# Windowed attention and two gated products on one core: scores three units ahead, weight conversions placed behind later landings, last output tile in two halves

## The chip, the cores and the metric

One core of a Trainium2 chip. The metric is the time of one execution on the device in microseconds, lower is better; three runs of the kernel before took 643.66 to 646.2 us, median 645.15.

## What is computed

```python
def reference(q, k, v, n_global, n_local, moe_w_a, moe_w_b, moe_w_out, moe2_w1, moe2_w2, moe2_w3, moe2_w_out):
    # q, k, v: (2, 8, 768, 64); n_global 8, n_local 96
    scores = q @ k.T / sqrt(64) - slope[h] * dist      # kept where global or in the last 96 keys
    a = softmax(where(keep, scores, -1e9))
    x = rows of (a @ v)                                # (1536, 512)
    x = (x @ w_a) * (x @ w_b) @ w_out                  # d_ff 1536
    return ((x @ w1) * (x @ w2) @ w3) @ w_out2         # d_ff 1024, out (1536, 512) float32
```

Only 104 earlier keys and the 128 of a query tile's own block can count, so a tile's scores are 232 wide, or 128 for the first tile of a batch.

## The kernel before

Weights reach the core as 64-bit floats and are turned into pairs of tiles, a high and a low part in TensorE's own 32-bit format; each product is three matmuls (high by high, high by low, low by high; lines 192 to 194).

**Attention** runs in 24 units (NU), a unit being four heads of one query tile of 128 rows. A unit passes scores (S, line 622 on PE), bias and row maximum (line 554 on VectorE), exponential with row sum (558, ScalarE), reciprocal (580, 581, VectorE), scaling (563, POOL), transposes (T, line 630 on PE), their copy out of PSUM, half by ScalarE (597) and half by VectorE (599), values (V, 641 on PE), and the split of the result into x high and x low (608 on ScalarE, 609 on VectorE). Twelve e tiles, two qk tiles, two vv tiles and one set of score banks serve all units. The first four units are 128 wide, the others 232. In step i of the generator `attention` (line 687) PE gets V of unit i-1, T of unit i and S of unit i+2; up to step 8 each for itself, after that the three in one block.

**Products.** x is cut into three chunks of 512 rows, eight units each. The first stage has six groups of 256 hidden columns, the second four. For a group and a chunk, `gate` makes 48 matmuls (two halves, weights A and B), `gated` forms the product on ScalarE and VectorE (721 to 729), and `down` makes 24 matmuls, whose results VectorE adds up (765). The order is chunk by chunk for groups 0 and 1, then group by group. The first product needs units 0 to 7 and weight A of group 0. In the second stage w3 and the last weight are multiplied first (`fold`, 24 matmuls, line 815), as they become ready.

**Weights.** `prep` (446) takes a raw buffer (three while attention lasts, two after it), loads 1 MB through SP's queue (455) and converts it: shift on VectorE (463), clamp on POOL (464), scale on ScalarE (465), two merges on VectorE (466, 468), high part on ScalarE (472), low part on VectorE (473), after which the buffer is free. Group 0 loads at once; group 1 when more than GP = 8 units have had their scores; later groups when attention has ended and their slot comes free.

**The order of work** is made beforehand by `Plan`, a list scheduler: every step is a strand that yields an engine, a planned duration and a time from which it is ready, and the planner always places the step that can start first, the lower rank first among equals (attention 8, a unit's softmax from 10 up, products 20, weights from 30 up). All instructions are then issued in order of their planned start, and each engine runs its own in that order. A load is planned at 3.1 us on the DMA engine plus 2.2 us; eight transposes at 0.1 + 0.87 x 2 = 1.84 us.

The last tile of each output is added up on VectorE and sent by SP's queue (777).

Of the kernel before, what the change touches and what calls it, by code (L numbers as in the profile page):

```python
# [10 lines left out]
I32 = mybir.dt.int32  # L11
AF = mybir.ActivationFunctionType
ALU = mybir.AluOpType
PSUM = bass.MemoryType.PSUM

P = 128
# [87 lines left out]
def op(eng, dur, ready, fn):  # L104
    return ((eng, dur),), ready, fn
# [3 lines left out]
def attention_moe_moe_kernel(  # L109
# [14 lines left out]
    nc = tc.nc  # L124
# [3 lines left out]
    B, NQ, _, NP, _ = qk.shape  # L128
    D = P // 2
    H = 2 * NP  # L130
    S = NQ * P
# [7 lines left out]
    CH = 512  # L139
    NC = NT // CH  # L140
# [242 lines left out]
    D_DVE = lambda n: 0.16 + 0.00104 * n  # L383
    D_MM = lambda n: 0.227 * n / 512
    LAT = 0.1
    PELAT = 0.25
    GP = 8
    with ExitStack() as fast:
        fast.enter_context(tc.manual_schedule())
        pl = Plan()  # L390
# [52 lines left out]
            return op("DMA", 3.1 * mb, 0.0, fn)  # L443


        def prep(src, shape, dst, key, gate=lambda: 0.0):

            yield gate
            i, t = yield from raw.get()
            buf = raw.tiles[i]  # L450
            if src.dtype == F32:
                w = buf.rearrange("p f w -> p (f w)")[:, 0:1024].bitcast(F32)
                t = (yield op("DMA", 1.6, t, lambda: nc.sync.dma_start(w.rearrange("p (a f) -> p a f", a=shape[0]), src))) + 2.2
            else:
                t = (yield op("DMA", 3.1, t, lambda: nc.sync.dma_start(
                    buf.rearrange("p f w -> p (f w)"), src.bitcast(I32).rearrange("p a f -> p (a f)")))) + 2.2
                low, top = buf[:, :, 0], buf[:, :, 1]
                tf = top.bitcast(F32)
                w = low.bitcast(F32)

                c = yield op("DVE", 0.75, t, lambda: nc.vector.tensor_scalar(low, low, 29, None, ALU.logical_shift_right))  # L463
                a = yield op("POOL", 1.2, t, lambda: nc.gpsimd.tensor_scalar(tf, tf, F64_MAX, -F64_MAX, ALU.min, ALU.max))  # L464
                a = yield op("ACT", D_ACT(1024), a + LAT, lambda: nc.scalar.activation(tf, tf, AF.Copy, scale=2.0 ** -112))  # L465
                c = yield op("DVE", 1.25, max(a, c) + LAT, lambda: nc.vector.scalar_tensor_tensor(  # L466
                    low, top, 3, low, ALU.logical_shift_left, ALU.bitwise_or))
                t = yield op("DVE", 1.25, c + LAT, lambda: nc.vector.scalar_tensor_tensor(  # L468
                    low, top, -0x80000000, low, ALU.bitwise_and, ALU.bitwise_or))
            w2 = w.rearrange("p (a f) -> p a f", a=shape[0])  # L470
            free = yield (lambda: slot_of(key))
            t = yield op("ACT", D_ACT(1024), max(t, free) + LAT, lambda: nc.scalar.activation(dst()[0], w2, AF.Copy))  # L472
            t = yield op("DVE", 1.25, t + LAT, lambda: nc.vector.tensor_tensor(  # L473
                dst()[1], w2, dst()[0].bitcast(F32), ALU.subtract))
            raw.free[i] = t + LAT
            ready[key] = t + LAT
# [26 lines left out]
            n0 = 2 if tag == "O" else KD  # L503
            return [s[:, 2 * k + z, :].rearrange("p (a f) -> p a f", a=n0) for z in range(2)]

        def prep_group(st, g, rank, gate=lambda: 0.0):
            for k, tag in enumerate("ABO" if st == 1 else "AB"):
                src = ((w_a, w_b, w_o) if st == 1 else (w_1, w_2))[k][g]
                pl.spawn(prep(src, (2, DM) if tag == "O" else (KD, 256), lambda tag=tag: slot(st, g, tag),
                              (tag, st, g), gate), rank)  # L510

        order = [(b, t) for t in range(NQ) for b in range(B)]
        NU = 2 * len(order)
        xr = {}
        att = {"began": 0, "done": 0, "end": 0.0}
        sS = [[bk[:, 0:2 * KW].rearrange("p (u k) -> p u k", u=2) for bk in bank[0:2]]][0]
        pts = bank[2:4]
        po = bank[4][:, 0:2 * P].rearrange("p (u k) -> p u k", u=2)  # L520
# [123 lines left out]
        def attention():  # L644

            def part(what, num):

                w, blocks = width(num)
                nb = len(blocks)
                if what == "S":  # L650
                    def r():
                        if ("q", num) not in ev or (num and ("ttr", num - 1) not in ev):
                            return None
                        return max(ev["q", num][1], ev.get(("ttr", num - 1), 0.0))

                    def then(t):
                        att["began"] += 1
                        if num % 2:
                            qkb.free[ev["q", num][0]] = t + LAT
                        pl.spawn(softmax(num, [t - 0.24 * nb + PELAT, t + PELAT]), 8)  # L660
                    return r, 0.3 + 0.34 * nb, lambda: scores(num), then
                if what == "T":
                    def r():
                        if ("e", num) not in ev or (num and ("pT", num - 1) not in ev):
                            return None
                        return max(ev["e", num][0], ev.get(("pT", num - 1), 0.0))

                    def then(t):
                        _, es, k = ev["e", num]
                        for ei in es:  # L670
                            eb.free[ei] = t + LAT
                        stb.free[k] = t
                        pl.spawn(evicted(num, [t - 0.44 * nb, t]), 9)
                    return r, 0.1 + 0.87 * nb, lambda: transposes(num), then

                def r():
                    if ("pT", num) not in ev or ("v", num) not in ev or (num and ("x", num - 1) not in ev):
                        return None
                    return max(ev["pT", num], ev["v", num][1], ev.get(("x", num - 1), 0.0))

                def then(t):
                    if num % 2:
                        vvb.free[ev["v", num][0]] = t + LAT
                    pl.spawn(rows(num, t), 9)
                return r, 0.2 + 0.54 * nb, lambda: values(num), then

            for i in range(-2, NU + 1):
                ps = [part(w, n) for w, n in (("V", i - 1), ("T", i), ("S", i + 2)) if 0 <= n < NU]
                whole = i > 8
                for k in range(1 if whole else len(ps)):  # L690
                    now = ps if whole else ps[k:k + 1]
                    t = 0.0
                    for x in now:
                        t = max(t, (yield x[0]))

                    def fn(now=now):
                        for x in now:
                            x[2]()

                    t = yield op("PE", sum(x[1] for x in now), t, fn)  # L700
                    for x in reversed(now):
                        x[3](t)
                        t -= x[1]
# [4 lines left out]
        accr = {}  # L708
# [46 lines left out]
        def added(st, g, c, m, k, t):  # L755

            last = g == (G1 if st == 1 else G2) - 1
            po = ybank.tiles[k]
            a = lambda: (accs[c] if c < 2 else late["acc"])[:, m, :]
            if g == 0:  # L760
                r = (yield lambda: late.get("t")) if c == 2 else 0.0
                r = max(r, accr.get((c, m), 0.0))
                u = yield op("ACT", D_ACT(CH), max(t + PELAT, r), lambda: nc.scalar.activation(a(), po, AF.Copy))
            else:
                u = yield op("DVE", D_DVE(CH), max(t + PELAT, accr[c, m]), lambda: nc.vector.tensor_tensor(a(), a(), po, ALU.add))  # L765
            ybank.free[k] = u + LAT
            accr[c, m] = u + LAT
            if last and st == 1:
                tok = slice(c * CH, (c + 1) * CH)
                u = yield op("ACT", D_ACT(CH), u + LAT, lambda: nc.scalar.activation(xh[:, m, tok], a(), AF.Copy))  # L770
                u = yield op("DVE", D_DVE(CH), u + LAT, lambda: nc.vector.tensor_tensor(
                    xl[:, m, tok], a(), xh[:, m, tok].bitcast(F32), ALU.subtract))
                xr[2, c, m] = accr[c, m] = u + LAT
            if last and st == 2:
                b, t = order[4 * c + m]
                row = (b * NQ + t) * P
                yield op("DMA", 0.8, u + LAT, lambda: nc.sync.dma_start(out[row:row + P, :], a()))
# [96 lines left out]
        pl.spawn(attention(), 8)  # L874
        pl.spawn(switch(), 0)
        prep_group(1, 0, 30)
        prep_group(1, 1, 31, lambda: 0.0 if att["began"] > GP else None)
        for g in range(2, G1):
            prep_group(1, g, 30 + g, lambda g=g: late.get("t") if ("A", 1, g - 2) in users else None)
            if g < 6:  # L880
# [17 lines left out]
    with tc.If(fv > 0):  # L898
        with ExitStack() as pg:
# [9 lines left out]
            for b in range(B):  # L909
                for p in range(NP):  # L910
# [9 lines left out]
                    for t in range(NQ):  # L920
# [12 lines left out]
                        po = gT.tile([P, P], F32, tag="O", name=f"o{nm}_{t}", bufs=1)  # L933
                        for j in range(2):
# [13 lines left out]
                            st = gs.tile([P, 4], F32, tag="st", name=f"st{nm}_{t}{j}")  # L948
# [14 lines left out]
        with ExitStack() as pg:  # L963
# [3 lines left out]
            f = ffn("g")  # L967
# [72 lines left out]
```

## Time and profile before

| | us |
|---|---|
| median of three runs | 645.15 |
| the profiled execution | 646.13 |
| its span in the trace | 644.2 |
| PE busy | 617.1 |
| DVE busy | 396.0 |
| ACT busy | 249.9 |
| POOL busy | 105.0 |

The span runs from the first to the last instruction; the 1.9 us to the execution's time lie around it. PE is TensorE, DVE VectorE, ACT ScalarE, SP the engine whose queue issues the loads. Lines (L622) are those of the kernel. A wait is put down to what came last before the waiting instruction. A busy row of several matmuls counts from the start of the first to the modelled end of the last, which overlaps the next by a little.

### The profile page before, as it was taken

What the parts mean: (1) busy time and instruction counts of PE and PEld (TensorE: products, weight loads), DVE (VectorE), ACT (ScalarE), POOL (GpSimd) and SP (SyncE); (2) the same over time, 40 slices, a digit from 0 to 9 for tenths busy, and PEclk for the clock granted to TensorE, in tenths of its full rate; (3) what the DMA queues carried; (4) which work ended last, traced back from release to release, by engine and by line L of the source; (5) the groups of instructions that cost most, each with busy time, mean ns of one, the idle gap of its engine ahead of it and who ended that gap; (6) DMA issues with size and microseconds to landing.
All of it is one profiled execution on the core that took longest, in us unless ns stands there. A gap on an engine that the chain in (4) does not pass through costs nothing.

```text
span 644.2 us, 8087 instructions
## 1 busy us (share of the span) xinstructions
PE 617.1 (96%) x3072; PEld 499.5 (78%) x3072; DVE 396.0 (61%) x693; ACT 249.9 (39%) x486; POOL 105.0 (16%) x149
## 2 busy tenths in 40 slices
PE   2788999999999999999999999999999999999996
PEld 1456777778888888888888888888888888888884
DVE  5979856555377997758788544981375276323333
ACT  4765766652244434413434223542452133111110
POOL 4645333330012121101111000110011010000000
PEclk9987999999999999999999999999999999999998
DMA  8454332320033433303333000420340030000012
GB/s 329 143 210 176 119 112 83 132 108 2 0 131 131 136 125 132 131 0 131 130 132 131 1 0 23 160 79 1 93 169 0 1 131 2 1 0 1 33 66 102
DMA packets 11647, 57.79 MB, mean 90 GB/s; under 512 B 1360, under 2 KB 2384, under 8 KB 6736
## 3 DMA queue, kind: packets, MB, share of 16 engines
q1 hardware_dynamic: 11456, 57.19, 25.4%
q8 instruction: 26, 0.43, 0.3%
q14 instruction: 21, 0.17, 0.1%
q10 hardware_dynamic: 144, 0.00, 0.0%
HBM read 54.04 MB, written 3.15 MB: 89 GB/s over the span
## 4 chain that ended last, share of the span: by engine, by line
PE 92%; DVE 3%; DMA 2%; POOL 1%; issue 1%; SPq 0%; ACT 0%; ACTq 0%
PE bank L192 28%; PE bank L194 28%; PE bank L193 28%; PE bank L630 3%; PE bank L641 3%; PE bank L622 2%; DMA raw<-in_moe_w_a_dram 2%; POOL e L563 1%; DVE e L554 1%; DVE st L580 1%; DVE raw L463 0%; SPq L529 0%; DVE slot L473 0%; DVE pT L599 0%; DVE acc L765 0%
## 5 line engine op out<-in xcount | busy, mean ns | idle before, releaser
L192 PE MATMUL bank<-xh,slot 128*128 128x512 f32 x480 | 188.3, 392 | 0.0
L193 PE MATMUL bank<-xl,slot 128*128 128x512 f32 x480 | 186.9, 389 | 0.0
L194 PE MATMUL bank<-xh,slot 128*128 128x512 f32 x480 | 186.8, 389 | 0.0
L464 POOL TENSOR_SCALAR raw<-raw 128x1024 f32<-128x1024 f32 x38 | 52.5, 1381 | 355.6 <-DMA raw<-in_moe_w_dram 157.4
L765 DVE TENSOR_TENSOR acc<-acc,bank 128x512 f32<-128x512 f32 x96 | 65.7, 684 | 70.0 <-PE bank L194 69.8
L192 PEld LDWEIGHTS bank<-xh,slot 128*128 128x128 f32 x480 | 90.2, 188 | 21.6 <-issue 3.2
L194 PEld LDWEIGHTS bank<-xh,slot 128*128 128x128 f32 x480 | 90.1, 188 | 19.0
L193 PEld LDWEIGHTS bank<-xl,slot 128*128 128x128 f32 x480 | 90.3, 188 | 18.3
L724 DVE TENSOR_TENSOR gt<-gt,bank 128x512 f32<-128x512 f32 x60 | 41.1, 684 | 68.5 <-PE bank L194 68.5
L728 ACT ACTIVATE gh<-gt 128x512 fp32r<-128x512 f32 x60 | 37.8, 630 | 115.1 <-DVE gt L724 115.1
L721 ACT ACTIVATE gt<-bank 128x512 f32<-128x512 f32 x60 | 35.8, 596 | 89.3 <-PE bank L194 89.1
L563 POOL TENSOR_SCALAR e<-e,st 128x232 f32<-128x232 f32 (+1 forms) x96 | 49.2, 531 | 65.3 <-DVE st L581 28.1
L465 ACT ACTIVATE raw<-raw 128x1024 f32<-128x1024 f32 x38 | 43.6, 1151 | 35.7 <-POOL raw L464 35.5
L192 PE MATMUL bank<-gh,slot 128*128 128x512 f32 x144 | 56.7, 394 | 0.0
L193 PE MATMUL bank<-gl,slot 128*128 128x512 f32 x144 | 56.2, 390 | 0.0
L194 PE MATMUL bank<-gh,slot 128*128 128x512 f32 x144 | 56.0, 389 | 0.0
L466 DVE SCALAR_TENSOR_TENSOR raw<-raw 128x1024 int32<-128x1024 int32 x38 | 47.8, 1259 | 9.2 <-ACT raw L465 8.8
L558 ACT ACTIVATE e<-e,st 128x232 f32<-128x232 f32 (+1 forms) x96 | 44.4, 464 | 21.3 <-DVE st L554 21.3
L729 DVE TENSOR_TENSOR gl<-gt,gh 128x512 fp32r<-128x512 f32 x60 | 44.9, 749 | 6.9 <-ACT gh L728 6.8
L468 DVE SCALAR_TENSOR_TENSOR raw<-raw 128x1024 int32<-128x1024 int32 x38 | 48.5, 1275 | 0.4
L472 ACT ACTIVATE slot<-raw 128x1024 fp32r<-128x1024 f32 x26 | 29.5, 1134 | 33.6 <-PE bank L193 23.8
L473 DVE TENSOR_TENSOR slot<-raw,slot 128x1024 fp32r<-128x1024 f32 x26 | 32.7, 1257 | 14.4 <-ACT slot L472 14.2
(67 smaller groups left out, 733.8 us busy)
## 6 DMA issues: line engine op xcount, KB each, us to landing
raw<-in_moe_w_dram SPq DMA_DIRECT2D x16, 1024.0 KB, 4.8
raw<-in_moe_w_out_dram SPq DMA_DIRECT2D x10, 1024.0 KB, 4.9
qk<-in_qk_dram SPq DMA_DIRECT2D x10, 720.0 KB, 4.2
raw<-in_moe_w_a_dram SPq DMA_DIRECT2D x6, 1024.0 KB, 5.6
raw<-in_moe_w_b_dram SPq DMA_DIRECT2D x6, 1024.0 KB, 6.5
vv<-in_vv_dram SPq DMA_DIRECT2D x10, 512.0 KB, 3.8
out_dram<-acc SPq DMA_DIRECT2D x12, 256.0 KB, 2.0
qk<-in_qk_dram SPq DMA_DIRECT2D x4, 256.0 KB, 4.1
```

The costliest lines, as they stand in the source:

```text
L192: nc.tensor.matmul(po, sh, mh, start=first, stop=False)
L193: nc.tensor.matmul(po, sh, ml, start=False, stop=False)
L194: nc.tensor.matmul(po, sl, mh, start=False, stop=last)
L464: a = yield op("POOL", 1.2, t, lambda: nc.gpsimd.tensor_scalar(tf, tf, F64_MAX, -F64_MAX, ALU.min, ALU.max))
L465: a = yield op("ACT", D_ACT(1024), a + LAT, lambda: nc.scalar.activation(tf, tf, AF.Copy, scale=2.0 ** -112))
L466: c = yield op("DVE", 1.25, max(a, c) + LAT, lambda: nc.vector.scalar_tensor_tensor(low, top, 3, low, ALU.logical_shift_left, ALU.bitwise_or))
L468: t = yield op("DVE", 1.25, c + LAT, lambda: nc.vector.scalar_tensor_tensor(low, top, -0x80000000, low, ALU.bitwise_and, ALU.bitwise_or))
L558: a = yield op("ACT", D_ACT(w) + 0.28, a + LAT, lambda: nc.scalar.activation(e, e, AF.Exp, bias=nmx, scale=-1.0, accum_out=sm))
L563: res["e"].append((yield op("POOL", 0.3 + 0.0011 * e.shape[1], r, lambda: nc.gpsimd.tensor_scalar(e, e, rs, 1.0, ALU.mult, ALU.mult))) + LAT)
L724: a = yield op("DVE", D_DVE(CH), max(a + LAT, pb), lambda: nc.vector.tensor_tensor(gt, gt, res["pB"], ALU.mult))
L729: a = yield op("DVE", D_DVE(CH), a + LAT, lambda: nc.vector.tensor_tensor(gl, gt, gh.bitcast(F32), ALU.subtract))
L765: u = yield op("DVE", D_DVE(CH), max(t + PELAT, accr[c, m]), lambda: nc.vector.tensor_tensor(a(), a(), po, ALU.add))
```

## The change

In `attention` PE gets S of unit i+3 in step i, and starts three units ahead. In `prep` a load of 64-bit weights is reckoned to land 5.5 us after its planned transfer instead of 2.2, and a new gate, `hold`, can keep the conversion back after the load. Group 1 uses it: its loads are no longer held, its conversions wait until GP = 7 units are through, and their rank is 12 instead of 31. In `added` the last output tile is added up and sent in two halves of 256 columns, the first by ScalarE's queue and the second by SP's.

```diff
--- before.py
+++ after.py
@@ -384,7 +384,7 @@
     D_MM = lambda n: 0.227 * n / 512
     LAT = 0.1
     PELAT = 0.25
-    GP = 8
+    GP = 7
     with ExitStack() as fast:
         fast.enter_context(tc.manual_schedule())
         pl = Plan()
@@ -443,7 +443,7 @@
             return op("DMA", 3.1 * mb, 0.0, fn)
 
 
-        def prep(src, shape, dst, key, gate=lambda: 0.0):
+        def prep(src, shape, dst, key, gate=lambda: 0.0, hold=lambda: 0.0):
 
             yield gate
             i, t = yield from raw.get()
@@ -453,7 +453,8 @@
                 t = (yield op("DMA", 1.6, t, lambda: nc.sync.dma_start(w.rearrange("p (a f) -> p a f", a=shape[0]), src))) + 2.2
             else:
                 t = (yield op("DMA", 3.1, t, lambda: nc.sync.dma_start(
-                    buf.rearrange("p f w -> p (f w)"), src.bitcast(I32).rearrange("p a f -> p (a f)")))) + 2.2
+                    buf.rearrange("p f w -> p (f w)"), src.bitcast(I32).rearrange("p a f -> p (a f)")))) + 5.5
+                yield hold
                 low, top = buf[:, :, 0], buf[:, :, 1]
                 tf = top.bitcast(F32)
                 w = low.bitcast(F32)
@@ -503,11 +504,11 @@
             n0 = 2 if tag == "O" else KD
             return [s[:, 2 * k + z, :].rearrange("p (a f) -> p a f", a=n0) for z in range(2)]
 
-        def prep_group(st, g, rank, gate=lambda: 0.0):
+        def prep_group(st, g, rank, gate=lambda: 0.0, hold=lambda: 0.0):
             for k, tag in enumerate("ABO" if st == 1 else "AB"):
                 src = ((w_a, w_b, w_o) if st == 1 else (w_1, w_2))[k][g]
                 pl.spawn(prep(src, (2, DM) if tag == "O" else (KD, 256), lambda tag=tag: slot(st, g, tag),
-                              (tag, st, g), gate), rank)
+                              (tag, st, g), gate, hold), rank)
 
 
 
@@ -684,8 +685,8 @@
                     pl.spawn(rows(num, t), 9)
                 return r, 0.2 + 0.54 * nb, lambda: values(num), then
 
-            for i in range(-2, NU + 1):
-                ps = [part(w, n) for w, n in (("V", i - 1), ("T", i), ("S", i + 2)) if 0 <= n < NU]
+            for i in range(-3, NU + 1):
+                ps = [part(w, n) for w, n in (("V", i - 1), ("T", i), ("S", i + 3)) if 0 <= n < NU]
                 whole = i > 8
                 for k in range(1 if whole else len(ps)):
                     now = ps if whole else ps[k:k + 1]
@@ -761,6 +762,17 @@
                 r = (yield lambda: late.get("t")) if c == 2 else 0.0
                 r = max(r, accr.get((c, m), 0.0))
                 u = yield op("ACT", D_ACT(CH), max(t + PELAT, r), lambda: nc.scalar.activation(a(), po, AF.Copy))
+            elif last and (st, c, m) == (2, NC - 1, 3):
+
+                b, n = order[4 * c + m]
+                row = (b * NQ + n) * P
+                for i in range(2):
+                    h = slice(i * (CH // 2), (i + 1) * (CH // 2))
+                    q = (nc.scalar, nc.sync)[i]
+                    u = yield op("DVE", D_DVE(CH // 2), max(t + PELAT, accr[c, m]), lambda h=h: nc.vector.tensor_tensor(
+                        a()[:, h], a()[:, h], po[:, h], ALU.add))
+                    yield op(("ACT", "DMA")[i], 0.3, u + LAT, lambda h=h, q=q: q.dma_start(out[row:row + P, h], a()[:, h]))
+                return
             else:
                 u = yield op("DVE", D_DVE(CH), max(t + PELAT, accr[c, m]), lambda: nc.vector.tensor_tensor(a(), a(), po, ALU.add))
             ybank.free[k] = u + LAT
@@ -874,7 +886,7 @@
         pl.spawn(attention(), 8)
         pl.spawn(switch(), 0)
         prep_group(1, 0, 30)
-        prep_group(1, 1, 31, lambda: 0.0 if att["began"] > GP else None)
+        prep_group(1, 1, 12, hold=lambda: 0.0 if att["done"] >= GP else None)
         for g in range(2, G1):
             prep_group(1, g, 30 + g, lambda g=g: late.get("t") if ("A", 1, g - 2) in users else None)
             if g < 6:
```

## Rows read from the trace of the kernel before

**Rows 1.** The page's first part: busy us, share of the span, instructions of each engine.

```profile
PE 617.1 (96%) x3072; PEld 499.5 (78%) x3072; DVE 396.0 (61%) x693; ACT 249.9 (39%) x486; POOL 105.0 (16%) x149
```

**Rows 2.** Table by stage: length, busy us (count) of PE, PEld, DVE, ACT, POOL; PEclk, DMA, GB/s.

```profile
9.60:46.20 36.60, 26.69 (x192) 17.74 (x192) 31.27 (x104) 25.93 (x85) 22.17 (x35) 0.95 0.57 206
...
50.80:55.60 4.80, 4.77 (x24) 3.48 (x24) 4.72 (x14) 3.95 (x12) 1.77 (x5) 0.50 0.67 262
...
55.60:142.60 87.00, 87.00 (x654) 66.63 (x652) 57.53 (x191) 54.58 (x162) 33.62 (x64) 1.00 0.33 109
...
56.00:80.00 24.00, 24.00 (x159) 18.64 (x159) 21.19 (x54) 15.94 (x43) 10.80 (x17) 0.99 0.30 96
...
142.60:632.00 489.40, 489.40 (x2160) 405.00 (x2159) 290.45 (x347) 159.14 (x214) 42.14 (x30) 1.00 0.20 69
```

**Rows 3.** What PE waited for: us in total, times, longest us.

```profile
PE bank L630 <- POOL e L563: 9.9, 6, 4.7
...
PE bank L641 <- DVE pT L599: 4.1, 2, 3.6
```

**Rows 4.** Timeline of DVE, 46 to 50.2 us: start us, us, instruction, idle before and releaser.

```profile
48.33 0.70 DVE L463 TENSOR_SCALAR raw<-raw 128x1024 int32<-128x1024 int32 x1 [2.11 <-DMA raw<-in_moe_w_a_dram]
...
48.94 1.05 DVE L580 TENSOR_SCALAR st<-st 128x4 f32<-128x4 f32 x1
...
50.12 0.66 DVE L599 COPY pT<-bank 128x512 f32<-128x512 f32 x1
```

**Rows 5.** Issue of group 1's first weight at 39.89 us: KB, us to landing.

```profile
raw<-in_moe_w_a_dram SPq DMA_DIRECT2D x1, 1024.0 KB, 8.4
```

**Rows 6.** Timeline of PE ahead of the first product and after it.

```profile
51.88 1.97 PE L630 MATMUL bank<-ident,e 128*128 128x128 f32 x8
...
53.78 1.92 PE L622 MATMUL bank<-qk 64*128 64x232 f32 x8
...
60.61 1.09 PE L630 MATMUL bank<-ident,e 128*128 128x128 f32 x8
...
61.63 1.05 PE L622 MATMUL bank<-qk 64*128 64x232 f32 x8
```

**Rows 7.** Timeline of PE, the first transposes.

```profile
13.47 0.83 PE L630 MATMUL bank<-ident,e 128*128 128x128 f32 x2 [4.74 <-POOL e L563]
```

**Rows 8.** Timeline of DVE, a hole behind the first transposes.

```profile
16.51 0.42 DVE L599 COPY pT<-bank 128x256 f32<-128x256 f32 x1 [1.07 <-PE bank L630]
```

**Rows 9.** Groups by line and shape, 0 to 56 us: busy us, mean ns, idle before.

```profile
L463 DVE TENSOR_SCALAR raw<-raw 128x1024 int32<-128x1024 int32 x4 | 2.9, 724 | 3.9 <-DMA raw<-in_moe_w_a_dram 3.5 <-DMA raw<-in_moe_w_b_dram 0.4
...
L466 DVE SCALAR_TENSOR_TENSOR raw<-raw 128x1024 int32<-128x1024 int32 x4 | 4.9, 1220 | 0.0
...
L468 DVE SCALAR_TENSOR_TENSOR raw<-raw 128x1024 int32<-128x1024 int32 x4 | 5.1, 1277 | 0.0
...
L554 DVE CUSTOM_DVE_ANT_0 e<-bank,tabs 128x232 f32<-128x232 f32 x25 | 8.7, 395 | 1.4 <-POOL e L563 1.1 <-PE bank L622 0.3
```

**Rows 10.** Timelines of DVE and ACT: a weight for a fold, and the fold's result.

```profile
413.89 1.22 DVE L473 TENSOR_TENSOR w3l<-raw,w3h 128x1024 fp32r<-128x1024 f32 x1
425.30 0.60 ACT L824 ACTIVATE slot<-bank 128x512 fp32r<-128x512 f32 x1 [1.48 <-PE bank L194]
```

**Rows 11.** The last add on DVE, its transfer's landing, the median of twelve.

```profile
638.02 0.69 DVE L765 TENSOR_TENSOR acc<-acc,bank 128x512 f32<-128x512 f32 x1 [0.67 <-PE bank L194]
out_dram<-acc SPq DMA_DIRECT2D x1, 256.0 KB, 3.8
out_dram<-acc SPq DMA_DIRECT2D x12, 256.0 KB, 2.0
```

**Rows 12.** Timelines of PE and DVE between two units at 100 us.

```profile
99.58 1.05 PE L622 MATMUL bank<-qk 64*128 64x232 f32 x8
...
99.69 0.69 DVE L599 COPY pT<-bank 128x512 f32<-128x512 f32 x1 [0.18 <-PE bank L630]
...
102.83 1.10 PE L641 MATMUL bank<-pT,vv 104*64 104x128 f32 x16
```

## The prediction

> **What bounds the kernel now.** I read the page's totals first [rows 1]: TensorE (PE) is busy 617 of 644 us, so only idle PE time and PE time at the lower clock can be won. The table by stage says where these lie [rows 2]: from 55.6 to 632 us PE is busy without a gap and at the full clock, and no edit can shorten that work. Everything worth having lies ahead of the first product, at 55.6 us, and in the last 6 us. The list of waits names what PE lacks there [rows 3]: scaled rows from POOL (9.9 us in six waits) and transposed tiles from VectorE (4.1 us, 3.6 of it in one wait). Last I followed VectorE (DVE) itself, because it feeds all of these: from 9.6 to 46.2 us it is busy 31.3 of 36.6 us [rows 2]. So attention up to unit 7, which the first product needs, is bound by VectorE with 5.3 us of holes in it, and not by PE.
>
> **Part 1: the conversion that waits for its transfer.** At 46.2 us VectorE stands still for 2.11 us at L463, the first step of converting group 1's first weight, because the plan reckons with 2.2 us after a transfer's own time and this load took 8.4 us to land [rows 4, 5]. Queued behind it on VectorE are the reciprocal (L580, L581) and the copy of the transposed tile (L599, at 50.12 us); PE waits for that copy, with nothing else in its queue that could run. After the change group 1 is loaded as soon as group 0 gives buffers back, its conversion is held until seven units are done, and every load is reckoned with 5.5 us. Without the wait, L463 (0.70) and the lengthened L580 (1.05) in front, the copy comes at about 46.5 and the wait of 3.6 us is all but gone: **-3.5** (between -3.5 and 0, the latter if another load or the released conversion stands there instead). Three DMA issues move forward on SP, past later qk and vv loads; where SP has to wait for a buffer of group 0, those loads wait with it. No such wait is in the trace; its bounds are 0 and 2.1 us, by the longest stall that a late load makes now [rows 4]. I take 0, because the buffers come free well before the units that need those loads, and their transfer is spread out, where now two weights are issued together.
>
> **The clock behind the gap.** The gap leaves PE at the lower of its two levels: granted 0.50 (1.2 GHz) from 50.8 to 55.6 us, behind that wait [rows 2]. The eight transposes there take 1.97 us and the eight score matmuls 1.92 us, against 1.09 and 1.05 a few us later [rows 6]: 1.75 us more, directly ahead of the first product. If the gap goes, this goes: **-1.8**; bounds 0 and -2.4 (half of the 4.77 us that PE was busy there).
>
> **Part 2: scores three units ahead.** No work is added: 24 units of scores either way, and the twelve e tiles still hold three units, since a fourth takes its tiles only once the transposes in front of it on PE have read them. What moves is the order. Now the third unit's scores stand on PE behind the first transposes, which wait for POOL until 13.47 us, and meanwhile VectorE idles [rows 7, 8]. With one unit more in hand, VectorE has a score tile to work on in those holes. Its holes sum to 5.3 us, so the gain is between 0 and that. Against it, the score op of one more unit (4 x 0.40 = 1.6 us [rows 9]) runs ahead of the first product; for it, PE has done 1.0 us more of its fixed work by then. That the later estimate also lets attention pass ahead of the first conversions is in the same holes. I take half the holes, 2.7, less 1.3 (the nearer spacing of the score ops, 0.32 each), plus 1.0: **-2.4**; bounds -6.3 and +0.6.
>
> **What is pushed back.** A conversion is four VectorE ops, 0.72 + 1.22 + 1.28 us and L473, as long as L466, together 4.4 us [rows 9]; a group has three. Of group 1, L463, L466 and L468 of the first weight (3.2 us) now lie ahead of the first product; they move behind it. From 56 to 80 us VectorE is busy 21.2 of 24 us already [rows 2], so 2.8 us are free there, and with products that start earlier the second group's weights are wanted earlier, 48 matmuls (10.9 us of PE) plus the attention between them after the first. PE waited for none of this before, so its cost is bounded by 0 and one whole conversion, 4.4 us. Between the ends I take **+2.0**, as the stretch is nearly full.
>
> **The other loads.** The larger estimate puts each later conversion up to 3.3 us back in the queues of VectorE, ScalarE and POOL. The tightest consumers are the folds: one weight is finished at 413.89 + 1.22 = 415.1 us; the fold's result is taken at 425.30, its 24 matmuls at 0.227 us (2160 in 489.4 us) make 5.4 us, so it starts near 419.8 [rows 10, 2]. 4.7 us of slack cover 3.3: **0**. If two delays add up in one buffer, 6.6 - 4.7 = 1.9 us for each of three such folds, 5.7 us at most.
>
> **The tail.** The last add takes 0.69 us and its transfer lands 3.8 us after it is issued, where the median of the twelve is 2.0 [rows 11]. Two halves on two queues let the first leave some 0.35 us sooner; the second leaves no sooner, since two halves cost more than one whole. Bounds: -1.8 (the median landing) and +0.4. I take **-0.2**. Speaking against it, the Trainium skill (DMA: Bandwidth & Descriptors, "Issuing engines are not separate DMA queues") says that transfers issued from several engines run on the same 16 DMA engines and save only the time to issue; by that the tail would bring 0 and the sum 639.4. No row here shows an output on two queues.
>
> **Sum.** -3.5 - 1.8 - 2.4 + 2.0 - 0.2 = -5.9 us. The profiled execution took 646.13 us (its span is 644.2), which gives 640.2; it lies 1.0 above the median of the runs, 645.15. Against the median the forecast is **639.2**.
>
> **Rivals.**
> *VectorE stays the bound (about 644).* The holes are not filled: part 2 costs 0.6, the pushed-back work 2.0, the clock gains nothing because PE still pauses just before the first product, and only the 3.5 stays: -0.9, so 644.2. For it: 31.3 of 36.6 us is already dense, and an L580 of 1.05 us [rows 4] shows what a neighbour on POOL can do to VectorE. Against it: the holes lie just where PE waits for POOL.
> *Holes all filled (about 634).* -3.5 - 2.4 - 6.3 and +1 give -11.2: 634. For it: POOL's six waits are 9.9 us, more than I credit.
> *Slower: attention too tight (650).* With more units in hand attention no longer pauses for its softmax, so the plan puts fewer matmuls between two units. Now 3.25 us lie between the end of a unit's transposes, where its scores begin (99.58), and the values that need their copy (102.83), and the copy is done at 100.38 [rows 12]. With the scores (1.0) and one step of three matmuls (0.7) between, 1.7 us are left; the copy needs 0.86, and with one conversion op (1.22) and one product op (0.69) ahead of it on VectorE 2.77, so PE waits 1.1 us, where before it never did. It ends slower by over 0.5% from nine such waits on (9.1 / 1.1); with ten it is 639.2 + 11 = 650. For it: group 1's conversions now fall into just this stretch, twelve ops of them. Against: the plan prices eight transposes at 1.84 us where they take 1.09 [rows 6], so what it thinks tight it mostly isn't on VectorE's side.
> *The edit doesn't act (645).* The hold opens once the seventh unit's rows are planned, so conversions could fill in where they stood; but the load is then long landed, so at least the stall goes.
>
> **How the numbers follow.** About 0.5% (3.2 us) is what a measurement of this kernel can tell from no change. The forecast, 637 to 642, has 0.52; the large gain 0.12; VectorE the bound 0.22; no effect 0.04; too tight 0.10. Faster is 0.52 + 0.12 less a sliver of the forecast above 641.9, 0.62; the same 0.28; slower 0.10. A range of 634 to 646 takes in all but the worst of the slower case and the far end of the large gain; it holds the bounds of part 2 and the pushed-back work when the others stand.
>
> **What would show it.** Right: the first product on PE near 48 us instead of 55.6; no wait of PE for L599 above 1 us before it; VectorE never waiting for a weight's load before 60 us; the third unit's scores before the first transposes; clock 1.00 in the 5 us ahead of the first product. Part 2 wrong: POOL's waits stay near 9.9 us, or VectorE's holes before 46 us do. Pushed-back work wrong: PE idle between the first product and the end of attention, at L641 for L599 (the slower rival) or at L192 for L473 (weights late). The fold cover wrong: PE idle near 420, 480 or 540 us. The whole would be wrong if attention's end and not the first product governed, or if the plan's reshuffled order put a new wait in PE's full stretch.

## The result: 630.0 us, a gain two and a half times the forecast

| | median us | lowest to highest | runs |
|---|---|---|---|
| before | 645.67 | 643.66 to 646.69 | 4 |
| after | 629.99 | 628.99 to 630.51 | 4 |

The ratio is 0.9759 (95% interval 0.9731 to 0.9787), 15.7 us less. The forecast was 639.2 in a range of 634 to 646: the sign was right, the size was not, and the time lies below the range. The profiled execution took 629.94 us, its span is 628.1.

The table by stage of the kernel after (length; busy us and count of PE, PEld, DVE, ACT, POOL; granted PE clock; DMA share; GB/s), one row up to the end of unit 7's split, one up to the end of attention, one of the full stretch behind it:

```profile
9.60:40.92 31.32, 28.67 (x234) 21.01 (x235) 28.16 (x118) 27.32 (x99) 23.95 (x42) 1.00 0.77 276
...
40.92:125.00 84.08, 83.34 (x634) 63.76 (x633) 66.38 (x201) 57.34 (x162) 40.03 (x62) 1.00 0.40 136
...
125.00:616.00 491.00, 491.00 (x2167) 406.73 (x2167) 280.95 (x345) 157.09 (x213) 37.33 (x30) 1.00 0.20 69
```

For the kernel before, the first of these stretches, to the end of the same split, is this row:

```profile
9.60:53.55 43.95, 30.14 (x216) 20.44 (x216) 36.47 (x119) 29.84 (x96) 25.51 (x40) 0.91 0.61 227
```

The reader is to see that PE does much the same work in both (30.1 and 28.7 us), that the stretch shrank from 43.95 to 31.32 us, and that VectorE's work in it shrank from 36.5 to 28.2. PE now fills 28.7 of 31.3 us, and the granted clock is 1.00 there instead of 0.91. What PE waited for in the whole kernel after (us, times, longest), to be held against [rows 3]:

```profile
PE bank L623 <- DVE st L555: 3.8, 3, 2.4
PE bank L623 <- DMA qk<-in_qk_dram: 3.5, 1, 3.5
PE bank L642 <- DVE xl L610: 1.1, 2, 0.5
PE bank L642 <- ACT pT L598: 0.5, 1, 0.5
...
PE bank L194 <- DVE slot L474: 0.2, 1, 0.2
```

POOL's 9.9 us are gone from the list, and so is the wait of 3.6 us for a transposed tile. From L463 on the lines of the kernel after are one higher (L463 is L464), from the output on twelve. The first product on PE comes at 40.36 us instead of 55.6; the last scores ahead of it take 1.05 us where they took 1.92 [rows 6]:

```profile
38.35 1.09 PE L631 MATMUL bank<-ident,e 128*128 128x128 f32 x8
39.38 1.05 PE L623 MATMUL bank<-qk 64*128 64x232 f32 x8
40.36 0.50 PE L192 MATMUL bank<-xh,slot 128*128 128x512 f32 x1
```

And the timeline of VectorE shows why (here only some rows: the conversions of 128x1024 and unit 7's split, L610):

```profile
11.86 0.66 DVE L464 TENSOR_SCALAR raw<-raw 128x1024 int32<-128x1024 int32 x1
...
31.83 1.25 DVE L474 TENSOR_TENSOR slot<-raw,slot 128x1024 fp32r<-128x1024 f32 x1
...
39.22 1.36 DVE L469 SCALAR_TENSOR_TENSOR raw<-raw 128x1024 int32<-128x1024 int32 x1
40.51 0.41 DVE L610 TENSOR_TENSOR xl<-bank,xh 128x256 fp32r<-128x256 f32 x1
...
43.80 1.21 DVE L474 TENSOR_TENSOR slot<-raw,slot 128x1024 fp32r<-128x1024 f32 x1
...
56.67 1.22 DVE L474 TENSOR_TENSOR slot<-raw,slot 128x1024 fp32r<-128x1024 f32 x1
```

The first weight of group 0 is finished at 33.1 us, the second only at 45.0 and the third at 57.9, both behind the first product. Before, all three were finished by 45.9, and two ops of group 1's first weight had followed as well. Counted in the timeline, 14 conversion ops stand ahead of unit 7's split before, 7 after.

### The profile page after: what moved, and what is told of

Same layout as the page of the kernel before. It is cut to its first block, busy times and chain, and to the rows that moved or that the text cites. A ratio compares the mean times of both kernels' runs of the same rounds, so it can differ in the third digit from the quotient of the medians.

```text
span 628.1 us, 8090 instructions
## 1 busy us (share of the span) xinstructions
PE 611.8 (97%) x3072; PEld 498.0 (79%) x3072; DVE 385.1 (61%) x694; ACT 247.0 (39%) x486; POOL 104.6 (17%) x149
## 4 chain that ended last, share of the span: by engine, by line
## 5 line engine op out<-in xcount | busy, mean ns | idle before, releaser
L465 POOL TENSOR_SCALAR raw<-raw 128x1024 f32<-128x1024 f32 x38 | 46.4, 1221 | 359.0 <-DMA raw<-in_moe_w_dram 131.9
L564 POOL TENSOR_SCALAR e<-e,st 128x232 f32<-128x232 f32 (+1 forms) x96 | 54.9, 589 | 46.6 <-DVE st L582 16.5
L730 DVE TENSOR_TENSOR gl<-gt,gh 128x512 fp32r<-128x512 f32 x60 | 43.5, 725 | 6.0 <-ACT gh L729 5.7
```

The source lines that it names most:

```text
L564: res["e"].append((yield op("POOL", 0.3 + 0.0011 * e.shape[1], r, lambda: nc.gpsimd.tensor_scalar(e, e, rs, 1.0, ALU.mult, ALU.mult))) + LAT)
L730: a = yield op("DVE", D_DVE(CH), a + LAT, lambda: nc.vector.tensor_tensor(gl, gt, gh.bitcast(F32), ALU.subtract))
```

## The experiments

All runs are judged by one account on VectorE: from 9.6 us to the end of unit 7's split, how many conversion ops are in it, how long VectorE is idle in it (the stretch less its busy time), and when PE's first product starts. The windows quoted below are these stretches.

| kernel | conversion ops | idle us | end of split | first product | median us | ratio (95%) |
|---|---|---|---|---|---|---|
| before | 14 | 7.5 | 53.55 | 55.63 | 645.67 | 1 |
| after | 7 | 3.2 | 40.92 | 40.36 | 629.99 | 0.9759 (0.9731 to 0.9787) |
| s3_only | 8 | 5.3 | 45.22 | 44.67 | 634.25 | 0.9835 (0.9801 to 0.9869) |
| no_s3 | 12 | 4.8 | 47.86 | 47.85 | 639.24 | 0.9924 (0.9895 to 0.9954) |
| o0b0_late | 6 | 7.8 | 44.13 | 47.16 | 640.60 | 0.9935 (0.9907 to 0.9963) |
| conv_first | 13 | 10.4 | 55.93 | 55.78 | 643.29 | 0.9972 (0.9952 to 0.9992) |
| no_lat | 8 | 3.6 | 43.14 | 43.11 | 632.72 | 0.9816 (0.9779 to 0.9852) |
| no_hold | 7 | 2.2 | 39.71 | 39.15 | 631.36 | 0.9797 (0.9759 to 0.9834) |
| no_tail | 7 | 2.3 | 39.79 | 39.23 | 630.13 | 0.9767 (0.9735 to 0.9800) |
| b0_late | 5 | 6.3 | 42.72 | 42.58 | 636.05 | 0.9854 (0.9817 to 0.9892) |
| lat_only | 12 | 6.7 | 49.68 | 49.69 | 640.17 | 0.9907 (0.9875 to 0.9938) |
| hold_only | 14 | 4.7 | 50.72 | 50.72 | 641.88 | 0.9953 (0.9927 to 0.9979) |
| s4 | 6 | 5.0 | 43.22 | 42.86 | 632.71 | 0.9807 (0.9760 to 0.9854) |

The kernel before ran beside each group of runs (medians 645.19, 645.58 and 646.00), and each ratio is to those. The kernel no_tail does the same as after until its last tile, and its split ends 1.1 us earlier: so differences of about 1 us between two profiled executions say nothing here.

### Scores three ahead alone (s3_only)

```diff
-            for i in range(-2, NU + 1):
+            for i in range(-3, NU + 1):
-                ... ("S", i + 2)) if 0 <= n < NU]
+                ... ("S", i + 3)) if 0 <= n < NU]
```

> The kernel before with one edit: scores three units ahead. Two theories. Queue theory: the first product waits for what the issue order puts on VectorE ahead of unit 7's last split; with scores three ahead the planner places attention in front of the conversions, 8 conversion ops of some 1.2 us stand there instead of 14, against 7 in the changed kernel: so nearly the whole gain, 631 to 633 us. Landing theory: the gain comes from conversions that no longer stand in front of transfers under way, which this edit does not touch: 642 to 645 us.

Measured 634.25 us, ratio 0.9835: 10.6 us of the gain from this edit alone, 1 to 3 us above the queue theory's time and far below the landing theory's.

```profile
9.60:45.22 35.62, 29.77 (x234) 21.31 (x235) 30.32 (x118) 28.45 (x100) 23.93 (x42) 1.00 0.73 247
...
44.67 0.50 PE L192 MATMUL bank<-xh,slot 128*128 128x512 f32 x1
```

Six ops are out of VectorE's stretch (5.7 us, each op counted to the start of the next) and its idle time fell from 7.5 to 5.3 us; shorter L580 rows and six small ops at L179 to L184 that now come later take off 1.5, four more score ops add 1.1. That is the 8.3 us by which the split moved. The granted clock rose with it, from 0.91 to 1.00. It is 1.00 here in every run with three or four units in hand except conv_first (0.74), and 0.87 to 0.92 in those with two; how much of the idle time the clock makes, no run separates. The 4 us that are still missing against after are one op, 2 us of idle time, and waits of PE behind the first product.

### The changed kernel with scores two ahead (no_s3)

```diff
-            for i in range(-3, NU + 1):
+            for i in range(-2, NU + 1):
-                ... ("S", i + 3)) if 0 <= n < NU]
+                ... ("S", i + 2)) if 0 <= n < NU]
```

> The changed kernel with scores two units ahead again, all else kept. 12 conversion ops stand ahead of unit 7's split instead of 7. Queue theory: five ops more, 5 x 1.2 = 6 us, 636 to 637 us. Landing theory: 630 to 632 us. If the units in hand matter by themselves (VectorE's holes while POOL and ScalarE finish a unit), the holes of 5 us come on top: 640 to 642 us.

Measured 639.24 us, 9 us above after (10.7 by the ratios): more than five ops alone, less than with all the holes; it lies between.

```profile
9.60:47.86 38.26, 29.77 (x225) 19.90 (x225) 33.43 (x118) 28.79 (x95) 24.71 (x40) 0.91 0.70 254
...
PE bank L631 <- POOL e L564: 7.0, 8, 1.8
```

Twelve ops and 4.8 us idle. PE's waits for POOL's scaling, absent from the list of after, are back with 7.0 us in eight waits.

### Few conversions ahead, but two units in hand (o0b0_late)

```diff
-        prep_group(1, 0, 30)
+        for k, tag in enumerate("ABO"):
+            pl.spawn(prep((w_a, w_b, w_o)[k][0], (2, DM) if tag == "O" else (KD, 256), lambda tag=tag: slot(1, 0, tag),
+                          (tag, 1, 0), hold=lambda tag=tag: 0.0 if tag not in "BO" or att["done"] >= GP else None), 30)
```

and scores two ahead, as in no_s3.

> The changed kernel with scores two units ahead again, and group 0's second and third weight held back until seven units are done, as group 1's are. 6 conversion ops stand ahead of unit 7's split, fewer than in the changed kernel, but with one unit less in hand. Queue theory: the first product as early as in the changed kernel, near 40 us, and 629 to 632 us. Units-in-hand theory: VectorE has holes while each unit's softmax goes round, so the first product comes near 45 us and the time is 634 to 638 us.

Measured 640.60 us, later than either theory said. It has the fewest ops of the runs with two units in hand, and yet:

```profile
9.60:44.13 34.53, 29.06 (x212) 19.43 (x212) 26.69 (x112) 25.66 (x92) 18.50 (x38) 0.90 0.69 253
...
PE bank L631 <- POOL e L564: 6.3, 7, 1.8
...
45.64 0.44 PE L631 MATMUL bank<-ident,e 128*128 128x128 f32 x2 [1.03 <-POOL e L564]
...
55.64 1.10 PE L642 MATMUL bank<-pT,vv 104*64 104x128 f32 x16 [1.02 <-DVE xl L610]
```

VectorE's idle time is 7.8 us: taking conversions away opened holes in their place, since with two units in hand the softmax's way round ScalarE and POOL isn't covered. The queue theory by itself has fallen here. So has the end of the split as the measure of the first product, which starts 3.0 us after it: transposes that stand ahead of it on PE wait three times for POOL, 2.6 us in all, and behind these waits the granted clock is 0.50 from 47 to 50 us. The second weight was then late too: PE waited for the conversions behind the first product.

### Three units in hand, conversions first (conv_first)

```diff
-        prep_group(1, 0, 30)
+        prep_group(1, 0, 5)
```

> The changed kernel with group 0's conversions ranked ahead of attention (rank 5 instead of 30), scores still three units ahead. 13 conversion ops stand ahead of unit 7's split instead of 7. Queue theory: 6 x 1.2 = 7 us later, 636 to 638 us. Units-in-hand theory: the holes take them in, 630 to 632 us.

Measured 643.29 us: 13 us above after, twice what the queue theory asked.

```profile
9.60:55.93 46.33, 31.61 (x233) 22.73 (x234) 35.97 (x128) 31.30 (x100) 24.50 (x44) 0.74 0.66 233
...
26.83 0.70 PE L642 MATMUL bank<-pT,vv 128*64 128x128 f32 x4 [7.04 <-DVE pT L600]
```

With the conversions ahead of it, attention stands in VectorE's queue (PE waits 7.04 us for one copy), the granted clock is 0.50 from 20 to 40 us, and three units in hand don't make up for it; what the third unit is worth in that order isn't measured, since no run has conversions first with two units. The runs so far say that the gain takes both, a third unit in hand and its work placed ahead of the conversions. The edit to the scores does both, because conversions rank behind attention and the planner gives them what time attention leaves.

### Without the later estimate (no_lat), without the hold (no_hold)

```diff
-                    buf..., src...)))) + 5.5
+                    buf..., src...)))) + 2.2
```

> The changed kernel with loads reckoned to land 2.2 us after their planned transfer again, instead of 5.5. Account theory: what sets the first product is, on VectorE ahead of unit 7's split, conversion work plus holes. 8 conversion ops stand there as in the run with scores three ahead alone, and that run's wait for the first weight's load (1.5 us on VectorE) comes back: 633 to 635 us. If group 1's hold is what keeps VectorE clear of loads, the estimate is worth nothing: 630 to 631 us.

Measured 632.72 us, 2.7 above after: just under the account's 633 to 635 and above the other theory's 630 to 631, though the two ratios' intervals overlap a little.

```profile
9.60:43.14 33.54, 28.29 (x233) 20.18 (x233) 29.94 (x119) 27.87 (x98) 23.51 (x42) 1.00 0.74 257
...
PE bank L631 <- POOL e L564: 2.3, 2, 2.0
```

One op more, and one wait of PE of 2.0 us for POOL at the start, where the clamp of the first weight (10.41 to 12.00 us) stands ahead of the first scaling (12.42) again. VectorE's wait for that load is 0.8 us, not the 1.5 expected.

```diff
-    GP = 7
+    GP = 8
-        prep_group(1, 1, 12, hold=lambda: 0.0 if att["done"] >= GP else None)
+        prep_group(1, 1, 31, lambda: 0.0 if att["began"] > GP else None)
```

> The changed kernel with group 1's loads gated as before (more than 8 units begun), no hold, rank 31. The issue order ahead of unit 7's split is the same as in the changed kernel, 7 conversion ops. Account theory: 629 to 631 us. If the early loads and the hold carry part of the gain (second group's weights in time), 632 to 635 us, with PE idle behind the first product for L474.

Measured 631.36 us, 1.4 above after; the two intervals overlap, so whether the hold is worth anything once the rest is there stays open. Behind the first product PE waits 2.9 us in this run, against 0.7 in after:

```profile
PE bank L642 <- DVE pT L600: 1.3, 1, 1.3
PE bank L642 <- DVE xl L610: 0.9, 1, 0.9
PE bank L642 <- ACT pT L598: 0.7, 1, 0.7
```

### The last tile whole (no_tail)

```diff
-            elif last and (st, c, m) == (2, NC - 1, 3):
+            elif False:
```

> The changed kernel with the last output tile added and sent whole. The trace of the changed kernel shows both halves landing 3.7 us after their issue, as the whole tile did (3.8), so splitting gave 0.2 us at most: 629.5 to 630.5 us. If the halves hide part of the landing: 631 to 632 us.

Measured 630.13 us: no difference that the runs can tell. In the trace of after both halves land 3.7 us after their issue, the second no sooner than the whole tile did [rows 11]:

```profile
622.10 0.75 DVE L772 TENSOR_TENSOR acc<-acc,bank 128x256 f32<-128x256 f32 x2 [0.67 <-PE bank L194]
...
out_dram<-acc ACTq DMA_DIRECT2D x1, 128.0 KB, 3.7
out_dram<-acc SPq DMA_DIRECT2D x1, 128.0 KB, 3.7
```

The Trainium skill (DMA: Bandwidth & Descriptors, "Issuing engines are not separate DMA queues") had it so: transfers issued by two engines run on the same 16 DMA engines, and only the time to issue is saved. The times agree, 630.13 beside 629.99 us and a landing after 3.7 beside 3.8; which DMA engines moved the halves these rows don't show.

### The other single edits (lat_only, hold_only)

lat_only is the kernel before with 5.5 for 2.2; hold_only is the kernel before with group 1's line and GP of the change.

> The kernel before with one edit: loads of 64-bit weights reckoned to land 5.5 us after their planned transfer instead of 2.2. 12 conversion ops stand ahead of unit 7's split instead of 14, and VectorE should wait for no load there (now 1.4, 0.4 and 2.1 us). Account theory: the 3.9 us of load waits and 2 ops of 1.2 us go, other holes take some of it back, as in the run with scores two ahead (639): 638 to 641 us. If only the one wait of 2.1 us counts, as PE's wait of 3.6 us says: 641 to 643 us.

> The kernel before with one edit: group 1's loads no longer gated, its conversions held until seven units are done, rank 12. 14 conversion ops still stand ahead of unit 7's split, but the load of group 1's first weight should have landed by then. Account theory: only PE's wait of 3.6 us for the copy behind that load, and the slow clock behind it, go: 639 to 642 us. If the load waits return elsewhere: 644 to 646 us.

Measured 640.17 us (0.9907) and 641.88 us (0.9953), both within the account.

```profile
9.60:49.68 40.08, 32.33 (x224) 21.71 (x224) 33.39 (x118) 28.89 (x95) 24.03 (x40) 0.87 0.63 238
...
9.60:50.72 41.12, 30.23 (x225) 20.32 (x225) 36.42 (x120) 30.20 (x96) 25.98 (x40) 0.92 0.67 247
...
PE bank L631 <- POOL e L564: 9.8, 7, 4.3
```

The first window is of lat_only, the other two rows are of hold_only: there POOL's waits stay where they were [rows 3] while the one wait behind the load is gone. By ratio the three edits bring 10.6, 6.0 and 3.0 us alone, 19.6 together, and 15.6 when made together: the later estimate and the hold remove in part what a third unit removes already. Taken out of the changed kernel they cost 2.7 (no_lat) and 1.4 (no_hold).

### Further the same way (b0_late, s4)

b0_late is the changed kernel with group 0's second and third weight held as in o0b0_late. s4 has scores four units ahead:

```diff
-        eb = Ring([at(f"e{i}", KW) for i in range(12)])
+        eb = Ring([at(f"e{i}", KW) for i in range(16)])
-        stb = Ring([... for i in range(4)])
+        stb = Ring([... for i in range(5)])
-            for i in range(-3, NU + 1):
+            for i in range(-4, NU + 1):
-                ... ("S", i + 3)) if 0 <= n < NU]
+                ... ("S", i + 4)) if 0 <= n < NU]
```

> The changed kernel with group 0's second and third weight held until seven units are done, as group 1 is. 5 conversion ops stand ahead of unit 7's split instead of 7. Account theory: first product 2 x 1.2 = 2.4 us earlier, near 38 us, if no hole opens in their place, and then 627 to 629 us. Rival: the second weight is wanted 2.7 us of matmuls after the first product and is late; PE waits for L474 or runs attention alone, and the time is 630 to 633 us.

> The changed kernel with scores four units ahead, 16 e tiles and five small statistic tiles instead of 12 and four. 6 conversion ops stand ahead of unit 7's split instead of 7. Account theory: in the changed kernel PE is busy 28.7 of the 31.3 us ahead of the first product, so at most some 2.6 us are left there: 628 to 630 us. If what is pushed behind the first product is then late, as in the run that held group 0's second weight back: 632 to 636 us.

Measured 636.05 and 632.71 us: neither beats the changed kernel. In b0_late the rival came true and more:

```profile
9.60:42.72 33.12, 30.14 (x233) 21.81 (x234) 26.81 (x122) 26.63 (x96) 21.14 (x43) 1.00 0.74 263
...
50.97 0.66 PE L642 MATMUL bank<-pT,vv 104*64 104x128 f32 x8 [2.23 <-DVE xl L610]
...
53.66 1.97 PE L631 MATMUL bank<-ident,e 128*128 128x128 f32 x8
55.56 1.92 PE L623 MATMUL bank<-qk 64*128 64x232 f32 x8
```

Two ops less, 3.1 us more idle: VectorE was no longer the limit there. And the conversions held back crowd behind the first product, where PE now waits 2.23 us for a split and 0.99 for a copy. Behind these waits PE runs at the lower of its two levels, granted 0.50 from 52 to 58 us: the last two rows take 1.97 and 1.92 us where the same ops took 1.09 and 1.05 in after. So the 6 us of this run are a first product 2.2 us later, 2.5 us more waiting behind it, and the clock for most of the rest (1.75 us in these two rows). In s4 VectorE is idle for 5.0 us and the scores of the fifth unit wait 1.1 us for the load of their qk tile; the interval overlaps that of after:

```profile
9.60:43.22 33.62, 29.71 (x242) 21.62 (x243) 28.59 (x132) 29.79 (x108) 24.27 (x46) 1.00 0.69 245
...
15.05 1.92 PE L623 MATMUL bank<-qk 64*128 64x232 f32 x8 [1.09 <-DMA qk<-in_qk_dram]
```

## Why the prediction was wrong, step by step

**What bounds the kernel: right.** All of the gain lies ahead of the first product, which moved 15.3 us; the last matmul on PE moved 15.9 (it starts at 621.67 instead of 637.60; PE now does 248 matmuls ahead of the first product instead of 241, so less is left behind it). The stretch behind attention stayed full, and no fold waited: the cover of 4.7 us for the later loads held.

**Part 1: the mechanism right, the size a little high.** Forecast -3.5 for the wait and -1.8 for the clock behind it, 5.3 together. The hold alone brought 3.0 us by ratio (interval 1.4 to 4.7) and 4.9 us to the first product in its trace. The clock is 1.00 ahead of the first product in after, as forecast. The clock term took in the last stretch alone: in the kernel before, the granted clock is 0.83 from 30 to 40 us too, and PE's busy time ahead of the first product fell from 35.0 us (241 matmuls) to 31.1 (248). VectorE bounds that stretch, so what this is worth in time isn't shown.

**Part 2: the step that failed.** The prediction put the gain of the scores between 0 and VectorE's 5.3 us of holes, and said that what the later estimate lets pass ahead "is in the same holes". Both sentences take VectorE's work ahead of the first product as given, but for 3.2 us of group 1. It isn't given. The first product needs unit 7 and one weight; of the 13.3 us of group 0's conversions, the second weight's last op and all of the third weight can come later, and a planner that ranks conversions behind attention does put them later as soon as attention always has a unit ready. The account of the whole change: the end of the split moved by 12.6 us; 7 ops fewer are 6.7 us, each op counted to the start of the next, and the idle time fell by 4.3. The rest, 1.6, is L580, which is no longer lengthened [rows 4] (2.1), and six small ops at L179 to L184 that now come behind the split (0.6), less four more score ops (1.1). For the scores alone (s3_only) it is 5.7 us of ops and 2.2 of idle time: the terms that the prediction had, half the holes and the price of one more unit's score ops, came out near (2.2 for 2.7, and 1.1 for 1.3), and the 5.7 are the term that it put at nothing. Forecast were 2.4 us for the scores, with 6.3 as the bound; alone they brought 10.6, and taking them out of the changed kernel cost 9.2 (639.24 less 629.99, rounded). The later estimate, put at nothing ahead of the first product but for its one wait, brought 6.0 alone, with two ops fewer.

**What was pushed back: the sign right, the size wrong twice.** The ops moved behind the first product were not three but eight, five of them group 0's (seven if counted at the split); and their price was not 2.0 us but 0.7: behind the first product PE waits 0.5 us for a copy and 0.2 for a weight. Read from VectorE's 21.2 of 24 us [rows 2], the stretch looked full, and it is: from 40 to 60 us VectorE is now busy 19.7 of 20. But PE is busy for all 20. That the plan can do this because products need little of VectorE and attention much is a reading of its order, which no run tests by itself. b0_late shows where the room ends.

**The tail: near nothing, as forecast.** Forecast -0.2, measured 0.1 in that direction and not to be told from none.

**The rivals.** "VectorE stays the bound" fell with the holes. "Attention too tight" didn't happen in the changed kernel; its signature, PE waiting at L642 for a copy or a split while conversions crowd, is what b0_late and o0b0_late show. "Holes all filled (634)" was the nearest. It was too small for the same reason as part 2: it filled the holes around work that could itself be moved out. "The edit doesn't act" is out: seven ops moved behind the split.

## What to carry to other kernels

When an engine is the bound ahead of an event, first list which of its ops the event needs, and only then its idle time: work that is merely queued ahead of the event is part of the gain. More units in hand pay twice under a scheduler with ranks, since they fill the round trip and hold back what ranks lower; here fewer conversions with two units (o0b0_late) and three units behind the conversions (conv_first) gave little. And work pushed back has an end to its room: holding back two ops more cost 6 us, part of it through PE's clock, which fell behind the new waits.

## What the runs showed of the hardware

An op of VectorE or POOL can take about twice its time while the other engine works beside it. In the kernel after, four scalings on POOL take 1.76 us in one place and 4.10 in another:

```profile
58.37 4.10 POOL L564 TENSOR_SCALAR e<-e,st 128x232 f32<-128x232 f32 x4 [2.48 <-PE bank L631]
...
72.12 1.76 POOL L564 TENSOR_SCALAR e<-e,st 128x232 f32<-128x232 f32 x4 [3.34 <-DVE st L582]
```

In the first place VectorE does a shift and two merges beside them, among others; in the second a copy out of PSUM and score ops. And a merge on VectorE that took 1.25 us at 35.53 takes 2.15 beside a clamp on POOL:

```profile
48.71 1.15 POOL L465 TENSOR_SCALAR raw<-raw 128x1024 f32<-128x1024 f32 x1
...
48.79 2.15 DVE L467 SCALAR_TENSOR_TENSOR raw<-raw 128x1024 int32<-128x1024 int32 x1
```

All thirteen traces together show that the neighbour is needed. Of the conversion ops on VectorE that stand in a row of their own with no POOL instruction beside them, 289 shifts took 0.68 to 0.70 us, 719 merges 1.20 to 1.23 and 356 low parts 1.21 to 1.23, without an exception. Every one that took over 1.3 times its usual time ran beside a clamp on POOL: 90 of 150 shifts, 48 of 155 merges and 15 of 81 low parts, up to 1.65, 2.20 and 2.13 us. So it is with the lengthened L580: 258 alone took 0.14 to 0.17 us, and 13 of 23 beside a clamp took over 0.5, up to 1.08.

The Trainium skill (GPSIMD Engine Reference, "1. Specifications") says that the two share their interfaces to SBUF and contend when VectorE reads two inputs or runs in a two-port mode. The merges read two inputs, and the rows agree; in which mode the shifts ran no row shows, and no run took the clamp away from a given op.
